# Two attention layers, twice, on one core: PV with values as weights in more groups, group ends ahead of scores, zero matmuls by weighted activity, copies on GpSimd

## The chip, the cores and the metric

The kernel runs on one core of a Trainium2 chip. The metric is device time in microseconds (us) of one execution. TensorE (PE) multiplies, ScalarE (ACT) computes exponentials, VectorE (DVE) and GpSimd (POOL) do elementwise work, SyncE (SP) issues DMAs. They run side by side and wait for one another through semaphores.

## The reference

Four layers, A B A B, each x = x + layer(layernorm(x)), on 2048 tokens of 512 features and 32 heads of 16 features, all in bfloat16. The two A layers (and the two B layers) share their weights.

```python
# layer A: 4 segments s of 512 tokens, causal softmax inside the segment, a memory M, z from earlier segments
p = softmax(q_s @ k_s.T * scale + mask);  a_dot = p @ v_s
a_mem = phi(q_s) @ M / (phi(q_s) @ z + 1e-6)
o = g * a_mem + (1 - g) * a_dot;  M += phi(k_s).T @ v_s;  z += sum(phi(k_s))
# layer B: softmax over all 2048 tokens
o = softmax(q @ k.T * scale) @ v
```

Each is followed by the product with wo. Nearly all the work is in the two B layers: 32 heads of 2048 x 2048 scores, each an exponential.

## The kernel before

The layers are numbered L = 0 to 3: 0 and 2 are A, 1 and 3 are B. The kernel's Python code plans the whole order ahead of time: `Sched` keeps, for each engine, a list of instructions and an estimate of when each ends, and `Builder` decides by these estimates what to issue next. Each engine runs its list in order.

**Groups and blocks.** A `Group` is four heads (of equal parity `e`, in one of four chunks `c` of 128 features) for one block of 512 queries. Its work is cut into blocks of 128 keys x 512 queries for one head: 64 blocks for a full B group (16 key blocks, four heads), 12 for an A group, 16 or so for a group that only sees one block of 512 keys. Layer 1 begins with partial groups (`waves`, queries 0 to 511, over one block of 512 keys each, as keys become ready), whose sums are kept in SBUF (`accS`), and goes on with 24 full groups (`first` and `last` both true) for the other 1536 queries. Layer 3 begins with partial groups over half of the keys each, some split further by `split`, and ends with 24 full groups. While groups of layer 1 run, the A groups of layer 2 for finished queries come in between.

**A unit.** The loop in `attention` goes unit by unit. `compose` takes three blocks; `unit` writes three score matmuls (32 contraction rows each, in three of the four row strips of the array, so that they run side by side) into one of two sets of three PSUM banks (`UNIT`), and one ACT exponential (line 1268) over all of them, whose result goes to a slot of `pT`. Two units later (three for A) `pv_step` multiplies these probabilities with the values and adds into the one accumulator bank (`ACC`). After compose and before or after pv_step, `background` runs pieces of other tasks: layernorm, projections, output products.

**Two ways to do PV** (`pv`). The usual way: the probabilities are the weights, 128 x 128, four times for a block, and the values with a column of ones stream through (34 or 51 columns). The `fm` way: 17 columns of values and ones are the weights, in one of the four 32-column strips of the array, and 512 columns of probabilities stream through, one matmul a block; blocks of different heads use different strips. `Group` sets `fm` from `FM`: 1 means full groups of layer 3 alone, 2 all groups of layer 3, 3 also full groups of layer 1. A group that is `fm` ends in `finish_fm`: a DVE transpose of the 128 x 512 accumulator to `tk` (line 1396), a reciprocal, a product, and every second group another DVE transpose to `oT` (line 1424, from `run_deferred`). One that is not ends in `finish`: a reciprocal (1366) and a product (1378), and the transpose is a DMA on SP's queue.

**Exponentials on DVE** (`dx`). Where `dx_room` allows, a block's scores go to DVE in place of ACT: `dx_first` (line 924) turns them into the bits of an approximate exponential, and `task_dx`, `dx_chain` make three copies with other offsets (line 970, two blocks in one instruction, 128 x 1024 uint16). All four versions go through PV, so such a block has four PV blocks instead of one. The results stand in work buffers: nine of its own and, once layer 0 is over (`wide`), areas of tensors that are no longer used (`dx_areas`): four more in layer 1, many more in layer 3. `dx_room` wants DVE's estimated end, with 350 ns for each copy still to do, before the unit's start plus `DQ`. `dxq` holds versions ready for PV, `PVN` and `PVLATE` say when PE takes them beyond what is due. With `POOL_ON` above zero a copy may go to POOL; at 0 none does.

**The group's end.** When a group's last block is due, `pv_step` does it and calls `pv_close`, or leaves the group in `pend` until its dx versions are through. The next group's PV cannot start before `finish` has read the accumulator.

**Zero matmuls.** The PE clock is gated by recent activity. `keep_busy` adds up to `FILLS` matmuls with zero weights a unit, while the activity by `streamed` (matmul time over the last 3413 ns, each weighted by the share of the array that it uses) is below `FILL`.

**POOL** makes `qm` (queries with the other parity's heads set to zero, line 1185) for B groups, and masks the exponentials of A groups (line 1283).

Of the kernel before, what the change touches and what calls it, by code (L numbers as in the profile page):

```python
# [25 lines left out]
LAG = {"pe": 100, "act": 60, "dve": 60, "pool": 70, "sp": 50}  # L26
# [51 lines left out]
class Sched:  # L78
# [1 line left out]

    CW = 0.5

    def __init__(self):
        self.ops = {e: [] for e in ENGS}
        self.t = {e: 0.0 for e in ENGS}
# [3 lines left out]

    def streamed(self, until, ns):

        while self.streams and self.streams[0][0] < until - ns:
            self.streams.pop(0)
        return sum(w for _, w in self.streams) / ns

    def estimate(self, op, ns, gap, tile):
        e = op.eng
        ready = max([d.end + LAG[d.eng] if d.eng != e else d.end + 35 for d in op.deps], default=0.0)  # L100
        if tile is not None:
            rows, r0, cols, c0, n = tile
            st = max(ready, self.pe_issue())
            if cols < 128:
                st = max(st, self.pe_issue() + 30)
            for (a, ar, b, bc, m, at) in self.tiles:
                if ar < r0 + rows and r0 < ar + a and bc < c0 + cols and c0 < bc + b:
                    st = max(st, at + m / 2.4 + (4 if (a, b) == (rows, cols) else 100))
            self.tiles = self.tiles[-11:] + [(rows, r0, cols, c0, n, st)]
            self.t["pe"] = max(self.t["pe"], st + n / 2.4)  # L110
            self.streams.append((st, n / 2.4 * rows / 128 * max(cols / 128, self.CW)))
            op.end = st + n / 2.4 + 170
        elif e == "sp":
            st = max(ready, self.t[e])
            self.t[e] = st + max(gap, 600)
            op.end = st + ns
        else:
            op.end = self.t[e] = max(self.t[e] + gap, ready + ns)
# [109 lines left out]
class Group:  # L228
# [4 lines left out]
    def __init__(self, L, kind, qseg, c, e, ksegs, first=True, last=True):  # L233
# [18 lines left out]
        self.started = set()  # L252
        self.fm = kind == "B" and Builder.FM >= (1 if L == 3 and first and last else 2 if L == 3 else 3 if first and last else 4)
        self.left = sum(1 if self.fm else sum(p[2] for p in PARTS[w]) // 128 if kind == "A" else 4 for w, q in self.banks)
# [4 lines left out]
class Builder:  # L259
# [3 lines left out]
    PART = 2  # L263
    FILL_DVE = 300
    EARLY = 200
    FILL, FILLS = 0.43, 2
    DVE_FIN, DX_FIN = 600, 2500
    EVAC_ACT = 0
    DX_BANK, DX_LATE, BG_BANK, DVE_LATE, DVE_LATE_LOW = 800, 3000, 200, 1500, 9000000000.0
    CR_A, CR_B, CR_W, CR_LOW, CARRY, CARRY_W, REST, NEAR, SLACK = 1300, 1500, 1400, 2200, 0, 0, 14, 10, 300  # L270
    ALT3, ALT5, GAP, AHEAD, PE_B, PE_A, PE_LOW, LOW, PAIRS, TAKEN, PAIRS2 = 2, 4, 3, 500, 4, 3, 4, 24, 60, 3, 1
    NKS = 6
    DX_T, POOL_T, POOL_ON = 430, 1800, 0
    DQN, TAKEN_N, REST_N, NEAR_N, NEAR_W = 600, 3, 14, 100, 24
    DQ, DXS, PVN, PVLATE, PVWAIT, PVHOLE = 3000, 4, 4, 600, 0, 100
    DMA_STEPS, DMA_LATE = 2, 300

    def __init__(self, nc, A_x, A_wq, A_wk, A_wv, A_wo, A_beta, B_x, B_wqkv, B_wo, out):
# [102 lines left out]
        return DmaBatch(self.dsems[self.ring("dsem", 1 << 30)])  # L381


    def keep_busy(self):


        g, n = self.cur, 0
        own = g is not None and g.npv
        if not own and (self.bank_late() > 0 or any(t["next"][0][:1] == ["cont"] for t in self.tasks)):
            return  # L390
        bank, al = (self.banks[ACC], g.acc) if own else (self.banks[DXB], self.new_alloc())
        while n < self.FILLS and self.sc.streamed(max(self.sc.t["pe"], self.sc.t["act"] - 1330), 3413) < self.FILL:
            self.mm(self.ps[:, bank.col0:bank.col0 + 512], self.zero[:, :], self.wB[:, 0, 0:512], not own, not own,
                    [self.b_zero, self.b_wB[0]], bank, al, "fill")
            n += 1
# [498 lines left out]
                self.dx_bufs.append(self.NDX + n)  # L894
                self.wide = True

    FM = 1
    NAREA, XDX = 38, 99

    def aslot(self, L, s):  # L900
# [51 lines left out]
    def dx_chain(self, k, b0, ents):  # L952


        n = 512 * len(ents)
        w = self.dx_space(b0)[:, 0:n]
        bw = self.b_dxw[b0][:len(ents)]
        hold = [b0] + [self.dx_bufs.pop(0) for _ in EXP_D[1:]]
        for j in range(1, len(EXP_D)):
            if j > 1:  # L960
                yield [], 0, self.DX_T
            b = hold[j]
            o, d = self.dx_space(b)[:, 0:n], float(EXP_D[j])
            wr = [x for i in range(len(ents)) for x in self.dx_writes(b, i)]
            ns = 435 if len(ents) == 2 else 333
            eng = "dve"
            if self.POOL_ON and self.wide and max(self.sc.t["pool"], bw[-1].last_write.end) + self.POOL_T < self.sc.t["dve"] + self.POOL_ON:
                eng, ns = "pool", self.POOL_T if len(ents) == 2 else 700
            self.dx_todo -= 1
            self.op(eng, (lambda o, d: lambda e: e.tensor_scalar(o, w, d, None, op0=ALU.add))(o, d), reads=bw, writes=wr, ns=ns, name="dxs")  # L970
            self.dx_queue(b, ents, j == len(EXP_D) - 1)
        self.dx_now[k] = []
        self.dx_done(b0)
# [533 lines left out]
    def attention(self):  # L1507
        self.flags = {("x", 0, s) for s in range(NSEG)}
        self.xT_free = [0, 1]
        self.dma_at, self.forcing = {}, False  # L1510
        self.sel, self.pvq, self.deferred, self.qm_free = [], [], [], [0, 1, 2, 3]
        self.qm_late = []

        self.dx_use, self.dx_bufs = [0] * (self.NDX + self.NAREA), list(range(self.NDX))
        self.areas, self.dx_open = self.dx_areas(), set()
        self.dx_build, self.dx_pairs, self.dx_now, self.dxq, self.dx_own = [], [], [[], []], [], []
        self.dx_seen, self.wide, self.dx_todo = set(), False, 0
        self.dx_step = self.bank_step = -9
        self.bubble = True
        self.forced, self.low, self.cur, self.gap = 0, True, None, 1  # L1520
        self.pend = None
        self.nfin, self.oT_owner = {}, {}
        self.cr_pe = self.cr_dve = 0
        self.step = self.bg_cols = 0
        self.misc_banks = [DXB]
        self.unit_no = 0
        self.parts = {}
        self.make_groups()
        self.make_tasks()
        n = 0  # L1530
        while True:
            items = self.take_banks(2)
            if not items:
                if not self.seqA and not self.seqB and len(self.tasks) == 2:
                    self.last_out(n)
                    break

                if self.pvq or self.pend:
                    self.step += 1
                    self.pv_step(n + 9, True)  # L1540
                    self.run_deferred(False)
                    continue
                self.misc_banks = [DXB, 0, 1, 2, 4, 5, 6]
                self.bubble = True
                if not self.bg_one():
                    assert self.deferred, ("stuck", [t["next"] for t in self.tasks])
                    self.run_deferred(True)
                continue
            self.misc_banks = [DXB]
            if self.bubble:  # L1550
                self.bubble, self.cr_pe, self.cr_dve = False, 0, 0
            self.step += 1
            self.near = self.ahead()
            self.dx_widen()
            self.low = self.near < self.LOW
            self.gap = self.GAP if self.near >= self.AHEAD else 1
            isA = items[0][0].kind == "A"
            split = not self.low and not isA
            self.unit_no = n
            self.units = n  # L1560
            self.compose(n, items)
            self.credit(self.PE_LOW if self.low else self.PE_A if isA else self.PE_B, self.CR_LOW if self.low else self.CR_A if isA else self.CR_W * len(items) / 3 if self.wide else self.CR_B)
            if split and (not self.FIT or not self.wide or self.FIT & 2):
                self.background(True)
            self.cr_dve -= self.pv_step(n)
            self.run_deferred(False)
            self.background(False if split and not (self.FIT & 1 and self.wide) else None)
            if self.step == 2:
                self.gates()
            left = sum(len(g.banks) - g.pos for g in self.sel)  # L1570
            if not self.seqA and not self.seqB and left <= 3 and not self.parts and len(self.tasks) == 2 and self.met([("dma", ("oT", 3, 3, c)) for c in range(NCH - 1)]):
                self.last_part(1, self.banks[DXB])
            elif self.step > 10:
                self.keep_busy()
            self.bg_cols = 0
            n += 1
# [49 lines left out]
```

## Time and profile before

| | |
|---|---|
| time, median of 3 runs | 1962.33 us (1961.81 to 1964.88) |
| the profiled execution's own time | 1963.52 us |
| its span (first to last instruction) | 1962.0 us, 64238 instructions |
| mean granted PE clock | 0.969 of full |
| busy: PE, PE weight loads (PEld) | 1752.8 us, 902.2 us |
| busy: DVE, ACT, POOL | 1523.5 us, 1822.8 us, 286.9 us |
| exponentials on ACT (line 1268) | 1612 instructions, 1793.1 us |
| DMA | mean 17 GB/s |

The stretches of the run can be told from the group ends on DVE (lines 1354, 1356, 1366, 1396): layer 0 and the waves of layer 1 until 451 us; full groups of layer 1 at 451 to 551, 592 to 692, 692 to 795, 836 to 938, 938 to 1041 and 1086 to 1178 us, four groups in each; the segments of layer 2 at 551 to 592, 795 to 836, 1041 to 1086 and 1260 to 1303 us; partial groups of layer 3 at 1178 to 1260 and 1303 to 1433 us; its 24 full groups from 1433 us to the end.

Busy time is an average: which engine limits is read in a stretch, from who waits for whom. A matmul's own duration says little, since matmuls are pipelined and those in different strips run side by side; the distance from one start to the next says more.

### The profile page before, as it was taken

The page shows a single profiled execution, that of the slowest core. Times are in us where ns is not written, and L with a number is a line of the kernel's source. Part 1 is how long each engine was busy: PE and PEld are TensorE (multiplying, and loading weights), DVE is VectorE, ACT ScalarE, POOL GpSimd, SP SyncE. Part 2 cuts the span into 40 slices and gives each one's busy share as a digit, 9 for nine tenths or more (in the row PEclk, how much of TensorE's full clock was granted, in tenths as well). Part 3 has the DMA queues.
Part 4 walks back from the last instruction along what each step waited for, and adds up shares of the span by engine and source line. Part 5 has one row for each costly group of instructions (what it writes and reads, how often), then busy time and mean ns, then how long its engine had stood idle before and what let it go on. Part 6 is the DMA issues. An engine that isn't in the chain of part 4 may idle for free.

```text
span 1962.0 us, 64238 instructions
## 1 busy us (share of the span) xinstructions
PE 1752.8 (89%) x28190; PEld 902.2 (46%) x28190; DVE 1523.5 (78%) x3240; ACT 1822.8 (93%) x1654; POOL 286.9 (15%) x648
## 2 busy tenths in 40 slices
PE   7889889899989999799998999899998888888887
PEld 3444444556646665466654666555632222222222
DVE  6656566788748797578875788577999999999996
ACT  6789988889999999999989999888999999999998
POOL 3522153110050000500004100231100000000000
PEclk9889998999999999999999899999999989999999
DMA  5110111000100010100011001010000000000000
GB/s 157 25 31 18 29 21 31 14 10 16 16 13 16 5 17 16 23 13 8 11 21 23 5 6 19 13 21 13 9 18 1 1 1 12 1 1 12 1 2 12
DMA packets 94968, 33.49 MB, mean 17 GB/s; under 512 B 87520, under 2 KB 94176, under 8 KB 94688
## 3 DMA queue, kind: packets, MB, share of 16 engines
q1 hardware_dynamic: 94688, 29.39, 7.6%
q8 instruction: 220, 3.60, 0.8%
q14 instruction: 60, 0.49, 0.1%
HBM read 6.30 MB, written 2.10 MB: 4 GB/s over the span
## 4 chain that ended last, share of the span: by engine, by line
PE 44%; ACT 27%; DVE 17%; issue 9%; DMA 1%; POOL 1%; SPq 0%; ACTq 0%; DVEq 0%; POOLq 0%
PE ps L398 44%; ACT pT L1268 26%; DVE dxw L924 3%; DVE dxw L970 2%; POOL pT L1283 1%; DMA xT<-xn 1%; DVE ob L1378 1%; DVE QA L924 1%; DVE VA L924 1%; DVE QA L970 1%; ACT amem L593 1%; DVE VA L970 1%; DVE KA L1396 1%; DVE wA L924 1%; DVE lnst L509 0%
## 5 line engine op out<-in xcount | busy, mean ns | idle before, releaser
L1268 ACT ACTIVATE pT<-ps 128x1536 bf16<-128x1536 f32 (+4 forms) x1612 | 1793.1, 1225 | 110.7 <-PE ps L398 89.3
L398 PE MATMUL ps<-qm,KB 32*128 32x512 bf16 x4096 | 540.4, 392 | 97.6 <-ACT pT L1268 82.1
L398 PEld LDWEIGHTS ps<-VB,pT 128*128 128x128 bf16 x8272 | 280.9, 97 | 217.9 <-issue 130.8
L398 PE MATMUL ps<-VB,pT 128*128 128x51 bf16 (+1 forms) x8272 | 353.7, 187 | 27.8 <-DVE ob L1378 9.9
L924 DVE TENSOR_SCALAR dxw<-ps 128x512 uint16<-128x512 f32 (+1 forms) x335 | 274.1, 821 | 63.2 <-PE ps L398 59.8
L398 PEld LDWEIGHTS ps<-qm,KB 32*128 32x128 bf16 x4096 | 133.8, 91 | 368.0 <-ACT pT L1268 269.5
L1283 POOL TENSOR_SCALAR_AFFINE_SELECT pT<-pT 128x256 bf16<-128x256 bf16 (+2 forms) x517 | 206.7, 419 | 564.2 <-ACT pT L1268 554.7
L1185 POOL TENSOR_SCALAR qm<-QB,par 128x512 bf16<-128x512 bf16 x88 | 73.7, 839 | 1018.2 <-PE ps L398 973.0
L398 PE MATMUL ps<-VB,dxw 128*128 128x51 bf16 (+1 forms) x5144 | 213.6, 186 | 0.4 <-DVE dxw L970 0.3
L398 PE MATMUL ps<-pT,VB 128*17 128x512 bf16 x1133 | 180.8, 391 | 10.7 <-DVE KA L1396 9.8
L398 PEld LDWEIGHTS ps<-VB,dxw 128*128 128x128 bf16 x5144 | 169.5, 96 | 4.5 <-issue 2.2
L970 DVE TENSOR_SCALAR dxw<-dxw 128x1024 uint16<-128x1024 uint16 (+1 forms) x363 | 144.7, 423 | 4.7 <-PE ps L398 3.4
L398 PE MATMUL ps<-qm,KA 32*128 32x128 bf16 (+3 forms) x1024 | 105.9, 313 | 35.6 <-ACT pT L1268 32.0
L398 PE MATMUL ps<-VA,pT 128*128 128x51 bf16 (+1 forms) x2560 | 116.8, 191 | 20.3 <-DVE ob L1378 14.2
L398 PEld LDWEIGHTS ps<-VA,pT 128*128 128x128 bf16 x2560 | 88.4, 98 | 81.6 <-POOL pT L1283 45.4
L398 PEld LDWEIGHTS ps<-pT,VB 128*17 128x17 bf16 x1133 | 41.4, 87 | 122.2 <-issue 103.5
L398 PE MATMUL ps<-dxw,VB 128*17 128x512 bf16 x338 | 93.9, 385 | 0.0
L398 PEld LDWEIGHTS ps<-qm,KA 32*128 32x128 bf16 x1024 | 29.7, 92 | 108.9 <-ACT pT L1268 78.8
L398 PE MATMUL ps<-wB,zero 128*128 128x512 bf16 x225 | 79.6, 411 | 0.0
L924 DVE TENSOR_SCALAR QA<-ps 128x512 uint16<-128x512 f32 (+1 forms) x67 | 59.8, 895 | 21.7 <-PE ps L398 21.1
L398 PE MATMUL ps<-xT,wA 128*128 128x512 bf16 x256 | 71.9, 393 | 2.7 <-DVE xT L555 0.9
L924 DVE TENSOR_SCALAR VA<-ps 128x512 uint16<-128x512 f32 (+1 forms) x75 | 65.2, 872 | 11.6 <-PE ps L398 11.0
(260 smaller groups left out, 2262.5 us busy)
## 6 DMA issues: line engine op xcount, KB each, us to landing
out_dram<-x SPq DMA_DIRECT2D x8, 256.0 KB, 2.2
x<-in_A_x_dram SPq DMA_DIRECT2D x3, 512.0 KB, 8.8
wB<-in_B_wqkv_dram SPq DMA_DIRECT2D x1, 1536.0 KB, 13.1
xT<-xn SPq DMA_TRANSPOSE x60, 2.5
oT<-ob SPq DMA_TRANSPOSE x52, 2.5
x<-in_A_x_dram SPq DMA_DIRECT2D x4, 128.0 KB, 2.2
wA<-in_A_wk_dram SPq DMA_DIRECT2D x1, 512.0 KB, 4.1
wA<-in_A_wq_dram SPq DMA_DIRECT2D x1, 512.0 KB, 5.3
```

What stands on the lines that cost most here:

```text
L398: self.sc.add("pe", lambda e: e.matmul(out, lhsT, rhs, start=start, stop=stop, skip_group_check=True), reads=reads, banks=[(bank, "w", all ...
L593: self.op("act", lambda e: e.activation(et, src, ACT.Exp), reads=bsrc, writes=self.b_amem, ns=1023, gap=915)
L924: self.sc.add("dve", lambda e: e.tensor_scalar(d, o, SCALE * LOG2E * 128, EXP_C, op0=ALU.mult, op1=ALU.add), writes=[w for j in range(k) f ...
L970: self.op(eng, (lambda o, d: lambda e: e.tensor_scalar(o, w, d, None, op0=ALU.add))(o, d), reads=bw, writes=wr, ns=ns, name="dxs")
L1185: self.op(eng, (lambda m, q, col: lambda e: e.tensor_scalar(m, q, col, 0.0, op0=ALU.mult, op1=ALU.add))(m, q, col), reads=[bq, self.b_par] ...
L1268: self.sc.add("act", (lambda dst, src: lambda e: e.activation(dst, src, ACT.Exp, scale=SCALE))(dst, src), writes=self.b_pT[slot * 3 + i:sl ...
L1283: self.op("pool", (lambda blk, pat: lambda e: e.affine_select(blk, blk, pattern=pat, compare_op=ALU.is_ge, fill=0.0, base=0, channel_multi ...
L1378: self.op("dve", lambda e: e.tensor_tensor(ob, src[:, :, 0:16], rb, ALU.mult), reads=[br] + bsrc, writes=[self.b_ob[oi][g.e]], bank=bk, al ...
L1396: self.op("dve", (lambda tk, a: lambda e: e.transpose(tk, a))(tk, src[:, sl]), reads=bsrc, writes=[self.b_tk] + extra, bank=bk, alloc=al, ...
```

## The change

`FM` goes from 1 to 3: partial groups of layer 3 and full groups of layer 1 become `fm` too. In the loop, when a group is pending or has its last block due in this unit, `pv_step` (and with it the group's end) comes ahead of `compose`, so PE gets these PV matmuls before the unit's scores. `streamed` weights matmuls with 0.285 for score matmuls, 0.38 for fm ones and 1 for all others (before: 0.25, 0.5 and 1), `FILL` is 0.5 instead of 0.43, and `keep_busy` looks at the window that ends where the next due probabilities are expected, where that is later. `POOL_ON` is 300: a copy goes to POOL if, at an assumed 2900 ns for 128 x 1024, it would end no later than 300 ns after DVE's estimated end. `DQ` is 2200 instead of 3000, `PVLATE` 900 instead of 600.

```diff
-    CW = 0.5
...
     def streamed(self, until, ns):
-        while self.streams and self.streams[0][0] < until - ns:
+        while self.streams and self.streams[0][0] < self.pe_issue() - 2 * ns:
             self.streams.pop(0)
-        return sum(w for _, w in self.streams) / ns
+        return sum(w for t, w in self.streams if t >= until - ns) / ns
...
-            self.streams.append((st, n / 2.4 * rows / 128 * max(cols / 128, self.CW)))
+            self.streams.append((st, n / 2.4 * (0.285 if rows < 128 else 0.38 if cols < 128 else 1)))
...
-    FILL, FILLS = 0.43, 2
+    FILL, FILLS = 0.5, 2
...
-    DX_T, POOL_T, POOL_ON = 430, 1800, 0
+    DX_T, POOL_T, POOL_ON = 430, 2900, 300
...
-    DQ, DXS, PVN, PVLATE, PVWAIT, PVHOLE = 3000, 4, 4, 600, 0, 100
+    DQ, DXS, PVN, PVLATE, PVWAIT, PVHOLE = 2200, 4, 4, 900, 0, 100
...
+    HOR = 0
+
     def keep_busy(self):
...
-        while n < self.FILLS and self.sc.streamed(max(self.sc.t["pe"], self.sc.t["act"] - 1330), 3413) < self.FILL:
+        soon = [w.end + LAG[w.eng] for e in self.pvq[:9] if e[0] <= self.unit_no + 1 for w in (self.b_pT[e[4] * 3 + e[5]].last_write,)]
+        at = max(self.sc.t["act"] - 1330, min(soon, default=0.0) - self.HOR)
+        while n < self.FILLS and self.sc.streamed(max(self.sc.t["pe"], at), 3413) < self.FILL:
...
-    FM = 1
+    FM = 3
...
-                eng, ns = "pool", self.POOL_T if len(ents) == 2 else 700
+                eng, ns = "pool", self.POOL_T * len(ents) // 2
...
             self.units = n
+            early = self.pend is not None or self.ends(0)
+            first = self.pv_step(n) if early else 0
             self.compose(n, items)
...
-            self.cr_dve -= self.pv_step(n)
+            self.cr_dve -= first if early else self.pv_step(n)
```

## The prediction

> **What bounds the kernel now.** I read the page's busy times, then busy time by the stretches of the table, then the timeline inside two of them, then groups and waits. Columns of the second fence: stretch, its length, then busy us and instructions of PE, PEld, DVE, ACT, POOL, granted clock.
>
> ```profile
> PE 1752.8 (89%) x28190; PEld 902.2 (46%) x28190; DVE 1523.5 (78%) x3240; ACT 1822.8 (93%) x1654; POOL 286.9 (15%) x648
> ```
> ```profile
> 592.00:692.00 100.00, 95.94 (x1993) 62.99 (x1993) 80.84 (x171) 95.57 (x83) 3.55 (x4) 1.00 0.07 11
> ...
> 1178.00:1260.00 82.00, 75.14 (x1489) 47.96 (x1489) 61.46 (x144) 74.91 (x65) 5.10 (x8) 0.96 0.10 17
> ...
> 1303.00:1433.00 130.00, 122.39 (x2483) 77.06 (x2483) 106.83 (x228) 119.38 (x102) 14.91 (x22) 0.99 0.05 11
> 1433.00:1957.00 524.00, 453.85 (x4356) 116.43 (x4353) 486.86 (x924) 514.92 (x449) 18.00 (x20) 0.98 0.02 5
> ```
>
> The end of layer 3, fm already, is bound by ACT (98%) and DVE (93%) together; a full group takes 524 / 24 = 21.8 us. Layer 1 at 592 to 692 us takes 25.0 us a group with DVE at 81%. ACT looks busy there too, but its exponentials are not back to back: 204 blocks (38 instructions of three, 45 of two) in 95.57 us are 0.468 us each, in layer 3 1130 blocks (232 and 217) in 514.92 us are 0.456. PE is what is full:
>
> ```profile
> 642.36 0.39 PE L398 MATMUL ps<-qm,KB 32*128 32x512 bf16 x3
> 642.68 0.48 PE L398 MATMUL ps<-VB,pT 128*128 128x34 bf16 x12
> 643.00 0.47 PE L398 MATMUL ps<-VB,dxw 128*128 128x34 bf16 x12
> 643.40 0.39 PE L398 MATMUL ps<-qm,KB 32*128 32x512 bf16 x3
> 643.72 0.60 PE L398 MATMUL ps<-xT,wB 128*128 128x512 bf16 x2
> 644.17 0.37 PE L398 MATMUL ps<-VB,pT 128*128 128x51 bf16 x8
> ```
> ```profile
> 1621.03 0.39 PE L398 MATMUL ps<-qm,KB 32*128 32x512 bf16 x3
> 1621.35 0.39 PE L398 MATMUL ps<-pT,VB 128*17 128x512 bf16 x2
> 1621.36 0.39 PE L398 MATMUL ps<-dxw,VB 128*17 128x512 bf16 x2
> 1621.58 0.38 PE L398 MATMUL ps<-phq,VB 128*17 128x512 bf16 x1
> ...
> 1621.90 0.39 PE L398 MATMUL ps<-qm,KB 32*128 32x512 bf16 x3
> ```
>
> From start to start: three scores 0.32 us, 24 usual PV matmuls 0.72 (0.030 each, 0.120 a PV block), two projection matmuls 0.45; in layer 3 eight fm blocks 0.55 (0.069 each), four 0.32.
>
> **The change part by part.** The sum is made against the profiled execution, 1963.5 us, which is 1.2 above the median.
>
> *Layer 1's full groups.* The stretch at 592 us holds 1672 PV matmuls (50 us of PE), 84 sets of scores (27), 64 projection matmuls (14): 91 of its 100 us. As fm it is 418 blocks at 0.075 (between 0.069 and 0.080), 31 us. One cost is new: usual PV and projections both use the whole array, fm PV doesn't. Three scores side by side need 0.21 (one set of four PV to the next, 1621.36 to 1621.58), yet 0.32 pass before the next kind, so a change of kind costs about 0.11; 32 pieces of projection make 3.5 us. PE then needs 27 + 31 + 14 + 3.5 = 76 of 100, and ACT ends last. The Trainium skill, TensorEngine Tiling (Array Packing), Key Properties, has this as a rule against the change: another tiling mode drains the engine. It gives no time; the 0.11 here agrees.
>
> The six layer-1 stretches are 600 us, 563.6 of ACT's 570.2 in exponentials, 1204 blocks at 0.468. At 0.456 these are 549, with 6.5 of other ACT work 555. ACT's share of layer 3 was 98%; with projections beside it I take 97%, between that and today's 95%: 572, a gain of **28**. Upper end, layer 3's pace: 24 x 21.8 = 524 us, plus what layer 1 has more. A DVE us costs 0.28 us when both engines are full (a dx block costs DVE 464 us of lines 924 and 970 / 396 blocks = 1.17, ACT 0.456: 0.85 / (0.85 + 2.19)). DVE's other work is 95 us in layer 1 (477 busy less 382 in these lines), with 25.6 more below, against 23 in layer 3: 27 us; ACT's 6.5 make 5. That is 556, a gain of 44. Lower end 10: PE's sets come out half empty.
>
> ```profile
> L1378 DVE TENSOR_TENSOR ob<-ps,rd 128x256 bf16<-128x256 f32 x88 | 37.3, 424 | 3.0
> ...
> L1396 DVE STREAM_TRANSPOSE KA<-ps 128x512 f32<-128x512 f32 x23 | 16.3, 709 | 0.8 <-PE ps L398 0.6
> ```
>
> The ends: 253 + 424 ns becomes 709 + 254 + 425 + 710 / 2 = 1743, 1.07 us more in 24 groups, 25.6 us of DVE. Its idle 123 us in these 600 hide it; without that cover, 25.6 x 0.28 = 7 us. 12 DMA transposes (2.5 us to landing) leave SP's queue; nothing waits long for them.
>
> *Partial groups of layer 3.* 212 us with PE at 93%, 408 blocks on ACT in 194 us. At 0.456 and 97%: 193, a gain of 19. But these groups also cover the wait for the last tokens' projections, so the lower end is 0; I take half, **10**. DVE: 24 copies or sums of 128 x 512 at 690 ns, not 430, and eight ends, 15 us, hidden by DVE's 44 idle us.
>
> *Group ends ahead of scores.* PE waits 48.7 us in all for DVE to have read the accumulator (24.0 for the product, 9.8 for the transpose, 14.9 for sums and copies); the 0.32 us of scores now fall into these waits. But scores stand behind the last PV, 0.3 to 0.7 us, and in A groups behind POOL's mask, for which PE's loads wait 45.4 us over 130 times. ACT's other bank set (1.03 us for two blocks) hides that; without it 10 us are lost. I take a gain of **3**, from a third of the 19.7 us that fall before 451 us and what layer 2 has; ends 15 and -10.
>
> *Zero matmuls.* 225 now, 0.21 us each. Weight 0.38 and threshold 0.5 ask for more. In layer 2's segments PE is at 81% and the clock at 0.90 to 0.96: room, and something to win. Half as many again are 24 us of PE, most of it idle time. Gain **2**, ends 10 and -8.
>
> *Copies on POOL, and DQ.* DVE copies start 0.335 us apart, so that is what a moved one frees. The trace has none on POOL; nearest is qm, 128 x 512, 692 ns undisturbed. Twice the width, some 1.3 us (estimate). It isn't free for DVE:
>
> ```profile
> 1561.41 0.42 DVE L970 TENSOR_SCALAR phq<-dxw 128x1024 uint16<-128x1024 uint16 x1
> 1561.74 0.84 DVE L970 TENSOR_SCALAR dxw<-dxw 128x1024 uint16<-128x1024 uint16 x1
> ```
> ```profile
> 1561.37 0.94 POOL L1185 TENSOR_SCALAR qm<-QB,par 128x512 bf16<-128x512 bf16 x1 [20.86 <-PE ps L398]
> ```
>
> A copy beside qm took 0.42 us more, and qm 0.25 more. The first halves (line 924, from PSUM) don't lengthen, so a long POOL copy can hide under them (1.2 us). The Trainium skill, SBUF — State Buffer, "SBUF: two separate sides", says that the two engines share a port pair which one instruction holds to its end while the other blocks. The rows agree; by the rule a waiting copy loses up to all of POOL's instruction. Between the 0.335 won and 0.1 to 0.5 lost on average I take **0** for the last stretch; for 150 copies there the ends are +0.3 and -0.25 us of DVE each, times 0.28, that is 13 and -10, and with DQ's shorter queue on a DVE at 93% a gain of 15 and a loss of 12. Behind a POOL copy on POOL's queue stand qm, made a group ahead, and the masks in layer 2, where POOL is two thirds busy.
>
> Sum: 28 + 10 + 3 + 2 + 0 = 43; 1963.5 - 43 = 1920.5, as a median **1919**.
>
> **The rivals.** *PE stays the bound.* Were fm blocks of one strip to follow each other, only two of four would run side by side: 418 x 0.108 = 45 us, PE needs 90 of 100 again. Gains 10 + 0 + 3 + 2: 1947. Against it: layer 3's sets of four.
>
> *Layer 3's pace everywhere.* PE, free, empties work buffers sooner, dx rises, POOL helps: 44 + 19 + 3 + 2 + 6 = 74: 1888. Against it: thirteen work buffers in layer 1, and projections.
>
> *Slower: POOL blocks DVE.* Place: DVE's copies from 451 us on. 1500 / 2.9 allows 517 POOL copies; say 300. If each holds back a DVE copy for 1.1 of its 1.3 us, DVE loses 0.765 net, 230 us, times 0.28 = 64: 1963.5 - 43 + 64, as a median 1983. It decides from 0.335 + 43 / (300 x 0.28) = 0.85 us each. For it: the port; against it: of qm's rows the worst DVE copy lost 0.62. By the skill's rule alone, an average wait is half of POOL's instruction, 0.65 (estimate).
>
> *No net change.* POOL at 0.85 each, or scores late behind group ends: 1962.
>
> **How the numbers follow.** Likeliest case 0.54 (own range 1905 to 1935), PE stays 0.17, layer 3's pace 0.13, slower 0.12, no net change 0.04. Faster by over 0.2% (what a measurement of this kernel can tell from no change): 0.84; within: 0.04; slower: 0.12. The range 1885 to 1962 leaves out the slower case, half of the fourth and about a third of the fast one.
>
> **What would show it.** Layer 1's groups at 23 to 24 us apart with PE below 88% busy, weight loads there down from 63% to some 25%, ACT at 97%; each group end there with a 0.71 us transpose; layer 3's last 24 groups at about 21.8 us still; POOL busy 200 to 500 us more. Wrong would be: DVE copies in layer 3 lengthened well past 0.42 us on average, PE waiting for POOL's copies, or layer 1 at 25 us a group.

## The result and the profile after

The changed kernel takes 2027.2 us (median of four runs, 2026.0 to 2036.5); the kernel before, on the same chip, 1963.6. The ratio is 1.033, 95% interval 1.030 to 1.037: slower by 3.3%. Forecast were 1919 us and a gain. The profiled execution took 2036.5 us, its span is 2034.6 us.

The first lines of the page of the changed kernel (to be held against the first fence of the prediction):

```profile
span 2034.6 us, 44576 instructions
PE 1761.4 (87%) x18191; PEld 599.6 (29%) x18191; DVE 1673.4 (82%) x2937; ACT 1824.5 (90%) x1658; POOL 1223.3 (60%) x979
```

PE's instructions fell from 28190 to 18191 and its weight loads from 902 to 600 us: fm is there. But DVE is busy 150 us longer, POOL 936 us longer, and ACT, with nearly the same exponentials to do, stands idle 71 us longer.

The time between group ends on DVE gives the stretches (us; in each row all parts of the kind are added up). The last two columns are experiments told below: POOL without copies, and fm alone.

| stretch | before | after | after, no POOL copies | before, fm alone |
|---|---|---|---|---|
| until layer 1's full groups | 451 | 439 | 430 | 446 |
| 24 full groups of layer 1 | 601 | 602 | 558 | 563 |
| segments of layer 2 | 170 | 184 | 175 | 192 |
| partial groups of layer 3 | 211 | 214 | 202 | 210 |
| 24 full groups of layer 3 | 522 | 588 | 524 | 527 |

Layer 1's full groups, where the gain was to come from, are no faster. Layer 3's, which fm and its order hardly touch, lost 66 us. Busy time in a stretch of layer 1 and in the end of layer 3, of the changed kernel (columns as in the prediction):

```profile
581.00:683.00 102.00, 92.89 (x750) 24.71 (x747) 89.27 (x156) 94.10 (x85) 58.53 (x27) 0.98 0.05 8
...
1440.00:2028.00 588.00, 493.56 (x4393) 123.48 (x4394) 557.45 (x754) 526.00 (x450) 481.74 (x183) 0.97 0.01 4
```

Weight loads in layer 1 are down to 24%, as forecast. In layer 3 DVE works 557 us instead of 487 with 754 instructions instead of 924, while POOL is busy for 482: DVE does less and takes longer. The copies (line 972) and POOL's, in the end of layer 3 (start, us, engine, line, tiles):

```profile
1642.62 0.41 DVE L972 TENSOR_SCALAR phk<-QA 128x1024 uint16<-128x1024 uint16 x1
1642.95 1.26 DVE L972 TENSOR_SCALAR dxw<-xT 128x1024 uint16<-128x1024 uint16 x1
...
1645.86 1.26 DVE L972 TENSOR_SCALAR phq<-xT 128x1024 uint16<-128x1024 uint16 x1
1647.04 0.41 DVE L972 TENSOR_SCALAR dxw<-KA 128x1024 uint16<-128x1024 uint16 x1
1647.38 0.41 DVE L972 TENSOR_SCALAR wA<-xT 128x1024 uint16<-128x1024 uint16 x1
```
```profile
1642.78 2.88 POOL L972 TENSOR_SCALAR phq<-xT 128x1024 uint16<-128x1024 uint16 x1 [0.68 <-DVE xT L926]
1645.74 2.94 POOL L972 TENSOR_SCALAR wA<-KA 128x1024 uint16<-128x1024 uint16 x1
```

A DVE copy that starts just after a POOL copy takes 1.26 us instead of 0.42 and ends some 1.4 us after POOL's start; two later ones run at full speed while the same POOL copy is still going. Over the whole trace 327 copies are on POOL, 2.86 us each; the 1014 left on DVE have a mean of 0.641 us (before: 1353 copies of 0.425), together 229 us above 0.42 each.

Who waited, before and after (engine, what waited, for whom: us in total, times, longest):

```profile
ACT pT L1268 <- PE ps L398: 89.3, 158, 4.7
```
```profile
ACT pT L1270 <- PE ps L400: 170.4, 286, 2.7
PEld ps L400 <- DVE dxw L972: 54.0, 97, 1.5
PEld ps L400 <- DVE dxw L926: 43.9, 83, 1.4
```

ACT waits for scores twice as long, because PE stands at PV matmuls whose copies DVE has not finished. Added over all rows, PE's matmuls wait 165 us for DVE (before 69), 101 of them for the approximate exponentials of lines 926 and 972 (before 6), and 5 us for POOL (before 5): POOL delivers in time, DVE doesn't.

### The profile page after: what moved, and what is told of

It reads as the page before. It is cut to its first block, busy times and chain, and to the rows that moved or that the text cites. A ratio compares the mean times of both kernels' runs of the same rounds, so it can differ in the third digit from the quotient of the medians.

```text
span 2034.6 us, 44576 instructions
## 1 busy us (share of the span) xinstructions
PE 1761.4 (87%) x18191; PEld 599.6 (29%) x18191; DVE 1673.4 (82%) x2937; ACT 1824.5 (90%) x1658; POOL 1223.3 (60%) x979
## 4 chain that ended last, share of the span: by engine, by line
DVE 45%; PE 28%; ACT 15%; issue 8%; POOL 2%; DMA 1%; ACTq 0%; DVEq 0%; SPq 0%; POOLq 0%
PE ps L400 28%; ACT pT L1270 15%; DVE dxw L972 7%; DVE dxw L926 6%; DVE QA L972 3%; DVE wA L972 2%; DVE VA L972 2%; DVE VA L926 2%; DVE QA L926 2%; DVE wA L926 1%; DVE KA L1398 1%; DVE xT L926 1%; DVE VB L972 1%; DVE KB L926 1%; DVE KB L972 1%
## 5 line engine op out<-in xcount | busy, mean ns | idle before, releaser
L400 PE MATMUL ps<-pT,VB 128*17 128x512 bf16 x2744 | 435.8, 393 | 31.2 <-DVE KA L1398 19.1
L400 PE MATMUL ps<-dxw,VB 128*17 128x512 bf16 x1464 | 331.4, 390 | 24.6 <-DVE dxw L972 19.4
L972 POOL TENSOR_SCALAR dxw<-dxw 128x1024 uint16<-128x1024 uint16 (+1 forms) x75 | 212.5, 2836 | 137.9 <-DVE dxw L926 123.4
L400 PE MATMUL ps<-QA,VB 128*17 128x512 bf16 x417 | 127.0, 389 | 11.2 <-DVE QA L972 10.8
L400 PE MATMUL ps<-VA,VB 128*17 128x512 bf16 x406 | 130.8, 397 | 5.7 <-DVE VA L972 4.1
L400 PE MATMUL ps<-qm,KA 32*128 32x384 bf16 (+3 forms) x1024 | 106.0, 316 | 32.9 <-ACT pT L1270 29.3
L972 POOL TENSOR_SCALAR dxw<-VA 128x1024 uint16<-128x1024 uint16 x30 | 86.0, 2866 | 23.5 <-DVE VA L926 22.6
L400 PEld LDWEIGHTS ps<-dxw,VB 128*17 128x17 bf16 x1464 | 70.5, 88 | 69.0 <-DVE dxw L972 50.4
L400 PE MATMUL ps<-wA,VB 128*17 128x512 bf16 x273 | 79.8, 403 | 1.7 <-DVE wA L972 1.0
L400 PE MATMUL ps<-VB,pT 128*128 128x51 bf16 (+1 forms) x1856 | 75.2, 189 | 6.6 <-DVE VB L1358 3.7
```

Source lines behind the costliest of these rows:

```text
L400: self.sc.add("pe", lambda e: e.matmul(out, lhsT, rhs, start=start, stop=stop, skip_group_check=True), reads=reads, banks=[(bank, "w", all ...
```

## The experiments

Two theories at first. *POOL*: the copies on POOL make DVE's copies longer than the plan says, and PE, whose order is fixed, waits. *Fm and order*: fm in layer 1 with its longer ends, or group ends ahead of scores, lose the time.

### POOL's copies taken away, and done alone

```diff
-    DX_T, POOL_T, POOL_ON = 430, 2900, 300
+    DX_T, POOL_T, POOL_ON = 430, 2900, 0
```

> The changed kernel with POOL_ON = 0, all else as changed: every copy on DVE again. Theory (POOL): the 327 copies on POOL free 327 x 0.335 = 110 us of DVE but lengthen the copies left on DVE by 229 us beyond 0.42 us each, and PE, in order, waits for them; without them the time falls to 1920 to 1945 us, DVE's copies are back at 0.42 us on average, and layer 1's full groups come at 24 us or less. Rival (fm and order): the loss sits in fm groups of layer 1 with their longer ends, and in the order of group ends; then the time stays above 1990.

Measured: 1901.4 us, 0.970 of before (0.968 to 0.972). POOL's copies cost 126 us, and the rest of the change gains 58 (the kernel before took 1959.7 us on the same chip). The page and a wait of this kernel:

```profile
PE 1688.8 (89%) x18183; PEld 584.4 (31%) x18183; DVE 1534.8 (81%) x3236; ACT 1806.2 (95%) x1666; POOL 287.4 (15%) x648
```
```profile
ACT pT L1270 <- PE ps L400: 51.6, 107, 1.8
```

All copies are on DVE again, and DVE is busy 139 us less than in the changed kernel. The time was 19 us better than my theory's best.

The other way round, on the kernel before:

```diff
-    DX_T, POOL_T, POOL_ON = 430, 1800, 0
+    DX_T, POOL_T, POOL_ON = 430, 2900, 300
...
-                eng, ns = "pool", self.POOL_T if len(ents) == 2 else 700
+                eng, ns = "pool", self.POOL_T * len(ents) // 2
```

> The kernel before with copies on POOL alone (POOL_ON = 300, POOL_T = 2900). Theory (POOL): slower than before by 30 us (DVE's net loss, some 0.36 us a copy times 0.28 times 300) to 75 us (with PE's waits): 1995 to 2040. Rival (fm and order): within 15 us of before.

Measured: 2098.8 us, 1.071 of before (1.069 to 1.073), more than either theory gave. Its page:

```profile
PE 1831.9 (87%) x28211; PEld 918.9 (44%) x28211; DVE 1645.8 (78%) x2940; ACT 1834.7 (87%) x1644; POOL 1150.3 (55%) x952
```

304 copies are on POOL; DVE is busy 122 us more, ACT's waits for PE's scores rise from 89 to 216 us, layer 3's end takes 604 us instead of 522. The second theory is out as the cause of the loss. Here 122 us of DVE go with 139 us of time, more than one for one; the granted clock is 0.936 against 0.969, and what part of the loss that makes stays open.

### Contention or late results

A POOL copy could also hurt by being late itself. So the order that took 1901 us was kept, every copy still on DVE, and POOL got work that nobody reads, where a copy would have gone:

```diff
+            if self.wide and len(ents) == 2 and max(self.sc.t["pool"], bw[-1].last_write.end) + self.POOL_T < self.sc.t["dve"] + 300:
+                s, c = self.KA[:, 1, 3, :].bitcast(dt.uint16), self.wB[:, 0, 0:512].bitcast(dt.uint16)
+                for _ in range(2):
+                    self.sc.add("pool", ... e.tensor_scalar(s, c, 22.0, None, op0=ALU.add) ..., deps=[bw[-1].last_write], ns=self.POOL_T // 2, name="dummy")
```

> The changed kernel without POOL copies (1901 us), its order unchanged on PE, ACT and DVE, and besides on POOL, at 296 places where a copy would have gone there, two copies of 128 x 512 uint16 from a weight tensor to an unused place, which nobody reads. The output stays the reference's. Contention: each of the 296 costs DVE 0.7 us as in the changed kernel, 207 us in all, and as no DVE work is taken away in return the time rises by 60 (at 0.28) to 210 us (all of it): 1960 to 2110; the unplanned-lateness theory says the upper half. Rival (PE waits for copies that POOL delivers late): nobody waits for these, the time stays within 15 us of 1901.

Measured: 2050.0 us, 1.046 of before (1.043 to 1.049), 149 us more than without. The page, the unread copies on POOL, and ACT's wait, in this kernel:

```profile
PE 1781.2 (87%) x18183; PEld 602.3 (29%) x18183; DVE 1710.6 (83%) x3236; ACT 1831.8 (89%) x1666; POOL 1249.3 (61%) x1240
```
```profile
L976 POOL TENSOR_SCALAR KA<-wB 128x512 uint16<-128x512 uint16 x592 | 960.0, 1622 | 429.8 <-DVE dxw L927 211.0 <-DVE VA L927 48.8 <-DVE QA L927 29.2
```
```profile
ACT pT L1276 <- PE ps L401: 172.4, 295, 3.5
```

DVE runs the very same 3236 instructions and is busy 1710.6 us instead of 1534.8; its copies take 0.557 us on average, the longest 0.875. PE's matmuls wait 159 us for DVE and 4 for POOL. Contention alone does it: 176 us of DVE became 149 us of time, 0.85 for one. The granted clock is lower too, 0.966 against 0.989; but the kernel with the old zero matmuls, further below, has 0.971 and takes 1906 us, so little of the 149 us can be put down to the clock.

### Unplanned lateness or the cost itself

My prediction had priced a DVE us at 0.28 us of time, since a slower DVE hands blocks to ACT. But the plan is made beforehand, with 435 ns a copy. Here it is told a longer time:

```diff
-            ns = 435 if len(ents) == 2 else 333
+            ns = (645 if self.wide else 435) if len(ents) == 2 else 333
```

> The changed kernel, its copies on POOL kept, but the plan is told that a pair's copy on DVE takes 645 ns from layer 1's full groups on (435 before; 646 is the mean that the changed kernel's trace shows). Theory A (unplanned lateness): the order of PE is fixed ahead by too short DVE times, so every us that DVE is late is waited out on PE; told the truth, the plan gives DVE fewer blocks, and what is left is DVE's net loss, 273 x 0.37 = 101 us, at 0.28: 1901 + 28, some 1930 (1915 to 1955). Theory B (the port's cost itself): it stays at 2000 or more.

Measured: 1954.7 us, 0.998 of before (0.996 to 1.000), with 273 copies on POOL. Of the 126 us, 72 are gone with most of the copies still there. Page and wait:

```profile
PE 1730.4 (89%) x18096; PEld 594.7 (30%) x18096; DVE 1603.3 (82%) x2903; ACT 1828.7 (94%) x1660; POOL 1073.4 (55%) x924
```
```profile
ACT pT L1270 <- PE ps L400: 81.8, 154, 2.3
```

ACT's wait for scores fell from 170 to 82 us; DVE now gets 843 blocks instead of 888. There are also 54 copies fewer on POOL; at 126 / 327 us each these alone would save some 21 us (an estimate), so about 51 of the 72 are the told plan's, half of what 273 copies would have cost. Yet 53 us remain against no POOL copies, not the 28 expected: ACT is busy 22.5 us longer, and waits 30 us longer. The 32 blocks that ACT has more make 15 of the 22.5, at 0.456 us each; the rest need not be work, since beside the unread copies the very same 1666 instructions of ACT were busy 25.6 us longer than without them. One reason for what remains may be that the plan knows only a mean, while a copy next to POOL takes 0.42 or up to 1.28 us; this was not tried. Theory B, 2000 or more, is out; theory A is right in part.

### Fm alone

```diff
-    FM = 1
+    FM = 3
```

> The kernel before with FM = 3 alone. Theory (POOL): fm alone gains as predicted, 28 + 10 us, some 1925 (1915 to 1945). Rival (fm and order): 1960 or more, with PE in layer 1 still over 93% busy or DVE in its place.

Measured: 1947.2 us, 0.993 of before (0.990 to 0.995): a gain, but 12 to 15 us, not 38. Layer 1's full groups gained what was forecast and more (601 to 563 us, in the table). The segments of layer 2 gave 22 back. A segment of layer 2 in this kernel, groups by cost:

```profile
L398 PE MATMUL ps<-xT,wB 128*128 128x512 bf16 x24 | 7.2, 419 | 0.3 <-DVE amem L682 0.3
...
L398 PE MATMUL ps<-wB,xT 128*128 128x512 bf16 x12 | 3.1, 379 | 0.6 <-DVE VB L425 0.6
...
L425 DVE CAST VB<-ps 128x512 bf16<-128x512 f32 x4 | 2.8, 690 | 4.5 <-PE ps L398 4.5
```

This is layer 3's projections at 1012 to 1064 us. Over the four segments there are 94 projection matmuls (of layers 2 and 3), before 36. They are background work; as layer 1's groups pass faster, fewer fit beside them, and the rest falls into segments where POOL's masks and short exponentials leave less cover. ACT's share of busy time there falls from 93% to 87%. But the segments don't all bear this out. By segment the projections are 20, 0, 36 and 38 (before 0, 0, 0 and 36), and the time grows by 3, 8, 7 and 5 us. The second, before and with fm alone (columns as above), has no projections in either:

```profile
795.00:836.00 41.00, 32.82 (x509) 16.96 (x509) 24.07 (x62) 38.83 (x44) 27.76 (x67) 0.95 0.13 28
```
```profile
817.00:866.00 49.00, 41.74 (x537) 20.16 (x532) 33.82 (x74) 42.35 (x46) 27.49 (x66) 0.77 0.15 21
```

It has other background work of layer 2 in it, DVE is busy 10 us longer, and the granted clock is 0.77 instead of 0.95; in the four it is 0.91, 0.77, 0.88 and 0.89, before 0.96, 0.95, 0.90 and 0.96. So displaced projections can stand for about 10 of the 22 us, those of the first and third segment; whether the rest is other displaced work or the lower clock stays open, and neither was tried by itself.

The same edit undone in the kernel of 1901 us:

```diff
-    FM = 3
+    FM = 1
```

> The changed kernel without POOL copies (1901 us), with FM = 1 as before. The prediction gave fm 28 us in layer 1 and 10 in layer 3's partial groups; on the kernel before, fm alone brought 12.5, with PE waiting for DVE's longer ends. If the predicted 38 us hold once group ends come first: 1930 to 1945, PE over 93% busy in layer 1's full groups. If fm is worth 12 here too: 1908 to 1918.

Measured: 1915.2 us, 0.976 of before (0.972 to 0.980). Fm is worth about 14 us here too: layer 1's full groups take 580 us without and 558 with it, layer 2's segments 169 and 175, layer 3's end 519 and 524.

### Group ends ahead of scores

Taken out of the kernel of 1901 us:

```diff
-            early = self.pend is not None or self.ends(0)
+            early = False
```

> As the kernel without POOL copies, and group ends again behind the scores. Prediction's step: the order is worth 3 us (15 to -10), so 3 us slower than with POOL_ON = 0 alone. Rival (fm and order): faster than that by 10 us or more.

Put into the kernel before, alone, and then with `FM = 3`:

```diff
+            early = self.pend is not None or self.ends(0)
+            first = self.pv_step(n) if early else 0
             self.compose(n, items)
...
-            self.cr_dve -= self.pv_step(n)
+            self.cr_dve -= first if early else self.pv_step(n)
```

> The kernel before with group ends ahead of scores alone. With POOL_ON = 0 that order was worth 44 us, not 3. If it works by itself: 1915 to 1935, mostly before 451 us and in layer 3. If only together with fm groups in layer 1 or with the new fills: 1950 or more.

> The kernel before with FM = 3 and group ends ahead of scores. If the two add up (12.5 and 44): 1907. What is left to 1901 is then zero matmuls, DQ and PVLATE. If they overlap: 1920 or more.

Measured: 1945.3 us (0.992 of before, 0.990 to 0.994), 1943.3 us (0.992, 0.989 to 0.994) and 1936.1 us (0.987, 0.985 to 0.990). The order is worth 18 us alone, 11 on top of fm, and 44 with everything else in place; the prediction had 3. PE's waits for DVE to read the accumulator, in the kernel before:

```profile
PE ps L398 <- DVE ob L1378: 24.0, 30, 2.8
PE ps L398 <- DVE KA L1396: 9.8, 20, 0.9
PE ps L398 <- DVE KB L1356: 6.3, 10, 1.3
```

and with the order changed alone:

```profile
PE ps L398 <- DVE ob L1378: 17.7, 20, 4.1
...
PE ps L398 <- DVE KB L1356: 0.3, 1, 0.3
```

With all tiles added, 51 us of such waits become 20; the transpose's wait is gone. In the profiled runs 15 us are won before 451 us and 13 in layer 1's full groups; some are given back later. By themselves fm and the order bring 31 us, together 25; the intervals are too wide to say whether they add up.

### What lies between 1936 and 1901

Left are the zero matmuls, `DQ` and `PVLATE`. Each was set back in the kernel of 1901 us: first the zero matmuls' weights, threshold and window, then `DQ` and `PVLATE` together (the last diff), then `DQ` alone of these two.

```diff
-            self.streams.append((st, n / 2.4 * (0.285 if rows < 128 else 0.38 if cols < 128 else 1)))
+            self.streams.append((st, n / 2.4 * rows / 128 * max(cols / 128, 0.5)))
...
-    FILL, FILLS = 0.5, 2
+    FILL, FILLS = 0.43, 2
...
-        at = max(self.sc.t["act"] - 1330, min(soon, default=0.0) - self.HOR)
+        at = self.sc.t["act"] - 1330
```
```diff
-    DQ, DXS, PVN, PVLATE, PVWAIT, PVHOLE = 2200, 4, 4, 900, 0, 100
+    DQ, DXS, PVN, PVLATE, PVWAIT, PVHOLE = 3000, 4, 4, 600, 0, 100
```

> The changed kernel without POOL copies (1901 us), with the weights, threshold and window of the zero matmuls as before. Fm and the order of group ends together gave 1936; what brings 1901 is the zero matmuls or DQ and PVLATE. If the zero matmuls (418 instead of some 200; granted clock 0.989 against 0.966): 1925 to 1935 here. If DQ and PVLATE: 1901 to 1910.

> The changed kernel without POOL copies, with DQ = 3000 and PVLATE = 600 as before. If the zero matmuls bring the 35 us: 1901 to 1910. If DQ and PVLATE do: 1925 to 1935.

> The changed kernel without POOL copies, with DQ = 3000 alone as before (PVLATE stays 900). If a shorter DVE queue is what helps, as slow as with both old values; if PVLATE is, 1901 to 1906.

Measured: 1905.7 us (0.970 of before, 0.967 to 0.974), 1923.2 us (0.980, 0.977 to 0.982), 1906.0 us (0.972, 0.970 to 0.974). The zero matmuls make no difference that can be told here, though there are twice as many and the granted clock is 0.989 with them against 0.971. Nor does `DQ` alone. With `PVLATE` back at 600 as well the time is 17 us longer than with `DQ` alone, more than the spread of the runs: that PE takes further dx versions only when the plan has it 900 ns ahead of ACT, not 600, counts, at least beside a `DQ` of 3000 (with 2200 it was not set back). ACT's wait for scores is 61 us with 900 and 70 with 600. The 4 us of the zero matmuls and the 22 of `DQ` and `PVLATE` make 26 of the 35 us; the rest is not told apart. The settings do not act by themselves: without the new order of group ends all of them together change nothing (1945 against 1947 us).

## Why the prediction was wrong

**The step that failed is "Copies on POOL, and DQ", priced at 0.** The copies cost 126 us; `DQ` by itself made no difference (1906 against 1901 us). For the copies each size was wrong.

- *Duration.* Twice qm's 692 ns was taken as 1.3 us. Measured are 2.86 us, near the 2900 ns that the change itself plans with and that the slower rival used to count copies. The smallest 128 x 512 uint16 copy takes 1.49 us, about twice qm of the same shape. The width was scaled; but qm is bfloat16 and a product with a value for each partition, the copy uint16 and a sum with a constant. Which of the two makes the difference no run shows.
- *DVE's loss.* 0.1 to 0.5 us a copy on average was assumed, against 0.335 freed. Measured: 229 us less the 9 that qm causes anyway, over 327 copies, 0.67 us. So DVE loses 0.34 us net for each copy that is taken from it, 110 us in all, and the first halves from PSUM give no full cover. (DVE's busy time grew by 139 us: it also got 888 blocks instead of 875, some 15 us at 1.17 each.)
- *What a DVE us costs.* 0.28 holds when work moves freely between DVE and ACT. The order here is fixed by estimates, so DVE's delay goes to PE and through the scores to ACT: 126 us for 139 us of DVE, 0.91. Cleanest is the 0.85 with the unread copies, where the order is the same; in the kernel before with POOL's copies alone it was 1.14. The told plan, which may rebalance, still paid 0.78 (53 us for 68.5).

With these the sum would have read 327 x 0.34 x 0.91 = 100 us of loss against the gains. The slower rival was the right mechanism, at 300 copies against 327; it decided from 0.85 us each at 0.28, but at 0.91 it decides from 0.335 + 43 / (327 x 0.91) = 0.48, and 0.67 is beyond that. It had each copy cost more than it did (1.1 us); its chance of 0.12 was too low mainly since the rate was wrong. Of the prediction's three signs of being wrong two came: DVE's copies lengthened to 0.641 us on average, and layer 1 stayed at 25 us a group. The third did not: PE waited for DVE's copies, not for POOL's.

**Layer 1's full groups, 28 us (10 to 44): right for the stretch, once POOL's copies are away.** Alone 38, undone 22. PE is free there, weight loads are at a quarter of the stretch, and ACT ends last: in the kernel without POOL copies it is busy 92.56 of 94 us:

```profile
565.00:659.00 94.00, 88.28 (x746) 23.69 (x745) 80.31 (x168) 92.56 (x82) 5.10 (x10) 1.00 0.04 8
```

What the sum lacked is what happens beside these groups: layer 2's segments lose 22 us with fm alone, 6 with the rest of the change, in part to projections that layer 1 no longer covers. PE stayed busier than forecast there (94%, not below 88%).

**Partial groups of layer 3, 10 us (0 to 19).** 9 in the kernel without POOL copies, 1 with fm alone, inside the ends.

**Group ends ahead of scores, 3 us (15 to -10): far too small**, 11 to 44. Only the waits before 451 us were counted, by a third. The gain isn't confined to that place: with the order alone, 13 us of it fall in layer 1's full groups, where PE is close to full and its lateness at a group's end goes on to ACT. What delayed scores cost is not shown by itself; it left a gain in all three cases.

**Zero matmuls, 2 us:** not distinguishable from nothing, inside the ends. `PVLATE` wasn't priced at all and is worth more.

Without POOL the prediction's own sum, 1919 us, was 18 us above what was measured, 1901. That it is so near is luck in part: fm brought some 14 us instead of 38, and the order of group ends and `PVLATE` made up for it.

## What to carry to other kernels

Before an operation is handed to another engine, price it by a row of the same operation, type and width, and count what it takes back from the engine that is relieved: here 0.335 us were freed and 0.67 lost for each copy. When the order is fixed ahead by estimates, a delay that the estimates don't know is paid nearly in full here (0.85 to 1.14), however much the engines could balance in principle; to tell contention from late results, keep the order and add work that nobody reads. A stretch that is sped up also covers less background work; look where that goes, segment by segment.

## What the runs showed of the hardware that I had not expected

A DVE copy beside a POOL copy isn't held up until POOL's instruction ends. Of the 218 DVE copies over 1.1 us in the changed kernel, 165 start 0.05 to 0.33 us after a POOL copy has begun and end 1.42 us (median) after its beginning, when it still has 1.45 us to go. The other 53 start 1.8 to 2.2 us into it and end 0.28 us after its end, such as this one beside a POOL copy that ends at 1377.62:

```profile
1376.65 1.25 DVE L972 TENSOR_SCALAR VA<-dxw 128x1024 uint16<-128x1024 uint16 x1
```
```profile
1374.60 3.02 POOL L972 TENSOR_SCALAR wA<-dxw 128x1024 uint16<-128x1024 uint16 x1
```

In between, 206 copies ran wholly inside a POOL copy in 0.45 us or less, nearly all of them starting 1.0 to 1.8 us into it. The longest took 1.29 us, 0.87 more than alone. The Trainium skill, SBUF — State Buffer, "SBUF: two separate sides", has the loser blocked for the whole instruction, and by it a wait of up to 2.9 us should have occurred; the runs look like two holds in one POOL copy, each worth a wait of up to 0.87 us, with a gap between. Beside the unread copies of 128 x 512, half as wide, the longest wait was 0.46 us, about half of it.
